# One bank and one place in the queue: value products, post-mix, pre-mix and scores of a talking-heads attention, reordered

## The chip, the cores and the metric

The kernel runs on one core of a Trainium2 chip. The metric is the device time of one execution in microseconds (us), the median of several runs. The kernel before takes 1507.99 us (three runs, 1506.14 to 1509.37). Times inside the program come from one further execution, recorded by the hardware profiler.

## The reference

Attention with heads mixed before and after the softmax ("talking heads"), followed by a small network that is linear but for one product of two halves:

```
scores = einsum('bhij,hg->bgij', q @ k^T / 8, w_pre)      # 8 batches, 12 heads, 448 x 448, head size 64
attn   = exp(scores - max) / (sum + 1e-9)
out    = einsum('bhij,hg->bgij', attn, w_post) @ v
x      = out as (8*448) x 768
result = (((x @ w1) * (x @ w2)) @ w3) @ w_out             # 768 -> 1024 -> 1024 -> 768
```

## The kernel before, in words

**Four products of the attention.** TensorE is used here as four 64 x 64 quadrants: two halves of its rows (the contraction) by two halves of its columns (the output partitions). A 4-byte float matmul shows in the profile as two instructions, so each product below counts twice there.

- *Scores* (`qk`, matmuls at L173): raw scores of a pair of heads, 128 queries by 448 keys; 8 instructions of 448 columns into two PSUM banks, 0 and 1 (6 and 7 for a second unit in one step). ScalarE copies the two banks out (L178, L179; in the first batch VectorE takes some) and SyncE stores them to DRAM (L184, L187). There the layout is changed: `fetch` (L201) reads rows back with (query, head) on the partitions.
- *Pre-mix* (`mix`, L219): a block of 5 queries x 12 heads = 60 partitions is multiplied with a 60 x 60 matrix that holds w_pre; 8 instructions of 448 columns into banks 2 and 3. One "set" is four such blocks, 20 queries; the 8 batches make 180 sets. VectorE takes the extreme of each row (`largest`, L226), ScalarE the exponential (`exp`, L234), both from banks 2 and 3.
- *Post-mix* (`post`, L259): the exponentials, 64 keys at a time, are the stationary operand, and the moving one is a 60 x 60 matrix with w_post and the softmax's denominators (`scale`: VectorE L243 and L244, GpSimd L246). 448 keys are seven tiles of 64. Key tile j of a block goes to PSUM partitions 0 to 63 where j is even and to 64 to 127 where j is odd, that is, to one column half of TensorE or the other. With two halves s of a set's queries and two blocks c that makes 28 products, 56 instructions of 60 columns, into banks 4 and 5, which hold 4 pairs of tiles (NJ = 4). The upper partitions beside the seventh tile are set to zero once, at the start (L781). ScalarE copies banks 4 and 5 out (`put`, L273) into `mt`, with the keys on the partitions.
- *Value products* (`av`, L300): `mt` times v, for 150 queries (a third of a batch) and three pairs of heads: 48 instructions of 150 columns (148 in the last third), which use all 128 rows and one column half each, into one bank, number 2. A batch has six such groups of three, the program 48. The padded v has 512 rows, with zeros in the last 64. In the third to eighth batch ScalarE copies the bank out (`leave`, L307, tile xd) and the result goes to DRAM; in the first two (`ONE = 2`) it is split at once into a rounded part (ScalarE, L321, tile xh) and a rest (VectorE, L322, tile xl).

**The network.** TensorE's remaining work, instructions of 128 x 128 by 448 columns in banks 6 and 7 (L359, L521, L552, L701), is dealt out over the steps by a table (`shares`), so that each step has about as much work on TensorE. It is called the experts' work below, as in the code.

**The order of the work** is written out by hand, and each engine runs its own instructions in that order. The loop in `run` makes half steps n; a set m has an even one (n = 2m: extremes, exponential) and an odd one (denominators). An odd half step's TensorE work is: experts, then value products if they are due (`avs`, in six of a batch's 22 or 23 odd steps), then a score unit if one is due (`qks`, in nearly all odd steps while a later batch is to come), then `post(m-1)`, then `mix(m+1)`, and then the next half step's experts. What leaves PSUM is put on lists: `ends` are run by `do_ends()`, `soon` by `do_soon()`, `later` (mostly DMAs) at the start of the next half step. `bank(i)` runs `ends` and `soon` first if something on them still has to read bank i. Score copies are issued inside `qk` itself; the copy out of the value products' bank is issued by the `do_ends()` that follows the value products and the scores.

All DMAs are issued by SyncE, in order. In an even half step `fetch` comes first, then what stands on `later`.

Of the kernel before, what the change touches and what calls it, by code (L numbers as in the profile page):

```python
# [6 lines left out]
F32 = mybir.dt.float32  # L7
# [3 lines left out]
ALU = mybir.AluOpType  # L11
# [4 lines left out]
B, H, S, D = 8, 12, 448, 64  # L16
DM, FF = 768, 1024
HP = H // 2
IB = 10
GI = H * IB  # L20
NB = -(-S // IB)
QT, NJ = 128, 4
GB = 15
# [3 lines left out]
HK = H * IH  # L27
PP = 64
JB = S // PP
# [20 lines left out]
class Kernel:  # L50
# [198 lines left out]
    def post(self, m):  # L249
        nc, w2s = self.nc, self.w2s.pop(m)  # L250
        if any(b in (4, 5) for b, _ in self.ends):
            self.do_ends()
        for s, e in enumerate(self.es.pop(m)[0]):
            for j in range(JB):
                a, z = divmod(j, 2)
                at = (2 * a + s) * HK
                for c in range(2):
                    k = slice(c * PP, c * PP + HK)
                    nc.tensor.matmul(self.pso[c][z * PP:(z + 1) * PP, at:at + HK], e[k, j * PP:(j + 1) * PP], w2s[k, s],  # L259
                                     start=True, stop=True)  # L260
        for c in range(2):
            n = 2 * m + c
            w, (b, t) = self.width(n), divmod(n, NB)
            a, u = divmod(t, GB)
            if u == 0:
                self.mt[b, a] = self.mp.tile([128, NJ, H, GB * IB], F32, tag="mt", name=f"mt{b}_{a}")
            src = self.pso[c][:, :NJ * 2 * HK].rearrange("p (j s g i) -> p j s g i", j=NJ, s=2, g=H)
            dst = self.mt[b, a][:, :, :, u * IB:u * IB + w]
            self.ends.append((4 + c, lambda dst=dst, src=src, w=w: self.put(dst, src, w)))
# [21 lines left out]
    def av(self, b, a, g):  # L291
        nc, cols = self.nc, self.cols(a)
        W = cols.stop - cols.start
        if g % 3 == 0:
            self.psa = self.bank(2, f"psa{b}_{a}_{g}")[:, :3 * GB * IB].rearrange("p (g i) -> p g i", g=3)
        v, mt = self.vs[b, g], self.mt[b, a]
        for j in range(NJ):
            for s in range(2):
                rows = slice(s * D, (s + 1) * D)
                nc.tensor.matmul(self.psa[rows, g % 3, :W], v[:, j, rows], mt[:, j, 2 * g + s, :W],  # L300
                                 start=(j == 0), stop=(j == NJ - 1))
        if g % 3 == 2 and b >= ONE:
            q, dst = self.psa[:, :, :W], self.x_d[b][g // 3][:, :, cols]
            x = self.xq.tile([128, 3, GB * IB], F32, tag="x", name=f"xd{b}_{a}_{g}")[:, :, :W]

            def leave():
                nc.scalar.copy(x, q)  # L307
                self.later.append(store)

            def store():  # L310
                nc.sync.dma_start(dst, x)
                self.x_made[b] += 1

            self.ends.append((2, leave))
        elif g % 3 == 2:
            if b not in self.xs:
                pool = self.xp[b % 2]
                self.xs[b] = [pool.tile([128, K1, S], F32R, tag=f"x{t}", name=f"x{t}{b}") for t in "hl"]
            h, l = (x[:, g - 2:g + 1, cols] for x in self.xs[b])
            q = self.psa[:, :, :W]  # L320
            self.ends.append((2, lambda: nc.scalar.copy(h, q)))  # L321
            self.soon.append((2, lambda: nc.vector.tensor_tensor(l, q, h.bitcast(F32), op=ALU.subtract)))  # L322
        if a == NG - 1:
            self.later.append(self.load_v)

# [414 lines left out]
    def run(self):  # L740
        nc, tc = self.nc, self.tc
# [36 lines left out]
        self.wpo = cp.tile([128, HK], F32, name="wpo")  # L778
        self.pso = [self.ps.tile([128, 512], F32, tag=f"b{4 + c}", name=f"pso{c}") for c in range(2)]
        for p in self.pso:  # L780
            nc.vector.memset(p[PP:, (NJ - 1) * 2 * HK:NJ * 2 * HK], 0.0)  # L781
        nc.sync.dma_start(self.wpo, self.wpost)
        fold_pieces = self.converting(self.fold_jobs())
        next(fold_pieces)
# [17 lines left out]
        loads, qks, avs = {}, {}, {}  # L802
# [83 lines left out]
        for n in range(N + 6):  # L886
            self.step, third = n, False
            if n == GB + 1:
                self.close("qp")
                self.xp = [self.pool("xp0", 1)]  # L890
            if n == SWITCH:
                assert done == total
                next(background, None)
                self.do_ends()
                self.do_soon()
                self.do_later()
                assert not fold_pieces
                self.close("fp")
                self.wp = self.pool("wp", 5, side="right")
                self.up = self.pool("up", 1, side="right")  # L900
                self.xp.append(self.pool("xp1", 1, side="right"))
                background, total, done = self.experts(phases), (E_1 + E_2) * ONE + P_1 * (B - ONE) // 2, 0
            if n == LATE:
                assert done >= E_1
                self.close("xp0", "cx")
                self.xq, self.cb = self.pool("xq", 2), self.pool("cb", 1)
            if n == PAIR:

                assert done >= 2 * E_1 + E_2 and unit_pieces is None and not self.jobs and not self.ys
                self.do_ends()  # L910
                self.do_soon()
                self.do_later()
                self.pairs, self.w_ahead = True, 4
                self.close("xp1", "cb", "xq", "cs")
                self.xq = self.pool("xq", 2)
                self.up2 = self.pool("up2", 1, side="right")
                self.free += range(N_UP, NS)
                setup = self.pair_setup(phases)
            if PAIR <= n < PAIR + 7:
                next(setup, None)  # L920
            m, odd = divmod(n, 2)
            if not odd and LF <= n + LF < N:
                self.fetch(m + LF // 2)
            self.do_later()
            if n + 3 < HP:
                others(n + 3)
            elif HP <= n < 2 * HP:
                self.load_v()
            for x in loads.get(n, []):
                self.load_kq(*x)  # L930

            p, pieces = self.n_made - 1 if fold_pieces else 2 * KF + 3 * KF, None
            if avs.get(n):
                pass
            elif fold_pieces:
                f = (self.n_made - 1 - 2 * KF) // 3
                if f < 2 or done >= 2 * KF * 3 * (f - 1):
                    pieces = fold_pieces
                    if next(pieces, self) is self:
                        fold_pieces = pieces = None  # L940
            if m < SETS:
                if odd:
                    self.scale(m)
                else:
                    self.largest(m)
            self.do_soon()
            if pieces:
                next(pieces)
            elif unit_pieces and not fold_pieces and not avs.get(n):
                ahead = 1 if n < SWITCH else 2 * done // (3 * K1) + 4 + (done > 0)  # L950
                if n_pieces < ahead:
                    n_pieces += 1
                    if next(unit_pieces, self) is self:
                        unit_pieces = None
                    else:
                        next(unit_pieces)
                        third = True
            now = share.get(n, 0)
            if n < SWITCH:

                wanted += now
                now = max(min(there(p), KF * 3 + wanted) - done, 0)
            self.do_sums()

            advance(now // 2)
            self.do_ends()
            if not odd and m < SETS:
                self.exp(m)
            advance(now - now // 2)
            for x in avs.get(n, []):  # L970
                self.av(*x)
            for i, x in enumerate(qks.get(n, [])):
                self.later.append(self.qk(*x, (6, 7) if i else (0, 1)))
            self.do_ends()
            if odd and 1 <= m <= SETS:
                self.post(m - 1)
            if odd and m + 1 < SETS:
                self.mix(m + 1)
            self.do_ends()
            if third:  # L980
                next(unit_pieces)

# [28 lines left out]
def layouts(inputs):  # L1011
# [4 lines left out]
    kq = np.ascontiguousarray(np.stack([qt.reshape(B, HP, 2 * D, S), kt], axis=3))  # L1016
    q0 = qt[0].reshape(HP, 2 * D, S)
    kq0 = np.ascontiguousarray(np.concatenate([q0[:, :, :QT], kt[0], q0[:, :, QT:]], axis=2))
    vv = np.zeros((B, HP, 2, NJ * 128, D), np.float32)
    vv[:, :, :, :S] = v.reshape(B, HP, 2, S, D)  # L1020
    vv = vv.reshape(B, HP, 2, NJ, 128, D).transpose(0, 1, 4, 3, 2, 5).reshape(B, HP, 128, NJ, 128)
    wpre = np.zeros((128, PP), np.float32)
    wpost = np.zeros((128, HK), np.float32)
# [26 lines left out]
```

## Time and profile before

| | |
|---|---|
| median of the runs | 1507.99 us |
| the profiled execution's own time | 1513.4 us |
| its span in the profile | 1511.6 us |
| TensorE matmuls busy | 1410.9 us, 93% |
| VectorE, ScalarE, GpSimd busy | 738.5, 831.1, 616.5 us |
| data moved | 416.85 MB, 276 GB/s in the mean |
| value products L300 | 2304 instructions, 292 ns each in the mean |
| post-mix L259 | 10080 instructions, 223 ns each |
| pre-mix L219 | 1440 instructions, 570 ns each |

How to read it: PE is TensorE's matmul queue, PEld its loading of stationary operands (which overlaps it), DVE is VectorE, ACT ScalarE, POOL GpSimd, SPq SyncE's queue of DMA issues. Instructions on PE overlap: the duration of one is from its start to its modelled end, and the pace is read from the distance of starts. In a timeline a row merges consecutive instructions of a line: start, length of the merged stretch, engine, line, operation, tiles, shape, count, and in brackets the idle time before it with what ended it. In the view of waits a row says who waited for whom: microseconds in total, times, longest.

### The profile page before, as it was taken

How to read it: one execution, taken by the hardware profiler on the slowest of the kernel's cores; microseconds unless marked ns; L12 is line 12 of the kernel's file. 1: busy time of each engine (PE TensorE's matmuls, PEld its weight loads, DVE VectorE, ACT ScalarE, POOL GpSimd, SP SyncE). 2: the span in 40 equal slices, each digit the busy share in tenths (PEclk: the TensorE clock that was granted, in tenths of full speed). 3: DMA queues.
4: the chain of work that ended last, by engine and by line, in shares of the span. 5: the costliest groups of instructions: out<-in, count | busy, mean ns of one | idle time of the engine just before them, and what ended most of it. 6: DMA issues, size and time to landing. Idle time of an engine off the chain costs nothing.

```text
span 1511.6 us, 45676 instructions
## 1 busy us (share of the span) xinstructions
PE 1410.9 (93%) x18684; PEld 1062.8 (70%) x18684; DVE 738.5 (49%) x1495; ACT 831.1 (55%) x1952; POOL 616.5 (41%) x754
## 2 busy tenths in 40 slices
PE   4869997999899989999999999999999999999999
PEld 1447775666677667667677777777777777899988
DVE  4756565667535443532334343443344447335573
ACT  3766565677656656665555665565555446532231
POOL 1322232344324444531243434543344337446683
PEclk8889999999999999999999999999999999999999
DMA  8988788898889998999988987889878757588875
GB/s 261 345 280 253 226 256 270 289 331 271 298 277 339 323 347 293 353 319 313 316 254 256 309 287 237 258 265 328 294 252 270 229 185 233 180 302 273 255 233 171
DMA packets 203759, 416.85 MB, mean 276 GB/s; under 512 B 20528, under 2 KB 120112, under 8 KB 203472
## 3 DMA queue, kind: packets, MB, share of 16 engines
q1 hardware_dynamic: 203552, 413.94, 83.7%
q8 instruction: 148, 2.42, 0.7%
q14 instruction: 59, 0.48, 0.1%
HBM read 279.77 MB, written 134.09 MB: 274 GB/s over the span
## 4 chain that ended last, share of the span: by engine, by line
PE 65%; DMA 13%; ACT 8%; issue 7%; DVE 5%; SPq 1%; POOL 0%; ACTq 0%; DVEq 0%; POOLq 0%
PE e L701 18%; PE psm L219 9%; PE psq L173 6%; PE pso L259 6%; PE psa L300 6%; PE psf L359 4%; PE e2o L701 4%; PE e3o L701 3%; PE eo L552 3%; PE e1o L701 3%; PE eg L521 3%; DMA wu<-w_d 2%; DMA raw_d<-st 2%; DMA s_d<-s 2%; ACT e L234 2%
## 5 line engine op out<-in xcount | busy, mean ns | idle before, releaser
L226 DVE TENSOR_REDUCE mn<-psm 128x1 f32<-128x448 f32 x360 | 207.9, 620 | 447.1 <-PE psm L219 446.8
L246 POOL TENSOR_SCALAR w<-wpo,ri 128x60 f32<-128x60 f32 x360 | 179.2, 515 | 542.8 <-DVE ri L244 522.0
L701 PE MATMUL e<-eh,wu 128*128 128x448 f32 x1008 | 298.2, 372 | 7.8 <-DVE c L655 4.6
L259 PEld LDWEIGHTS pso<-w,e 60*64 60x64 f32 x10080 | 204.4, 136 | 76.2 <-issue 68.1
L234 ACT ACTIVATE e<-psm,mn 128x448 f32<-128x448 f32 x360 | 226.0, 636 | 50.5 <-DVE mn L226 50.4
L178 ACT COPY st<-psq 128x448 f32<-128x448 f32 x162 | 86.5, 534 | 295.2 <-PE psq L173 135.3
L219 PE MATMUL psm<-r,wsc 60*64 60x448 f32 (+1 forms) x1440 | 199.1, 570 | 51.5 <-ACT xd L307 17.1
L273 ACT COPY mt<-pso 128x480 f32<-128x480 f32 x352 | 201.1, 638 | 67.0 <-PE pso L259 66.9
L701 PEld LDWEIGHTS e<-eh,wu 128*128 128x128 f32 x1008 | 188.0, 188 | 55.6 <-issue 29.5
L259 PE MATMUL pso<-w,e 60*64 60x60 f32 x10080 | 207.7, 223 | 0.5 <-issue 0.5
L701 PE MATMUL e<-el,wu 128*128 128x448 f32 x504 | 187.1, 371 | 0.0
L300 PE MATMUL psa<-mt,v 128*64 128x150 f32 (+1 forms) x2304 | 156.9, 292 | 3.9 <-ACT e L234 3.9
L173 PE MATMUL psq<-kq 64*64 64x448 f32 x1176 | 150.1, 571 | 8.2 <-ACT st L178 8.2
L300 PEld LDWEIGHTS psa<-mt,v 128*64 128x64 f32 x2304 | 143.6, 137 | 19.9 <-issue 9.5
L655 DVE TENSOR_TENSOR c<-c,e 128x448 f32<-128x448 f32 x168 | 101.5, 617 | 66.1 <-PE e L701 61.5
L521 PE MATMUL eg<-xh,wu 128*128 128x448 f32 x384 | 119.7, 381 | 4.3 <-DMA wu<-w_d 4.3
L640 POOL TENSOR_TENSOR el<-x,eh 128x448 fp32r<-128x448 f32 x90 | 104.2, 1176 | 32.7 <-ACT eh L639 29.2
L701 PEld LDWEIGHTS e<-el,wu 128*128 128x128 f32 x504 | 94.8, 188 | 22.7 <-issue 14.1
L521 PEld LDWEIGHTS eg<-xh,wu 128*128 128x128 f32 x384 | 71.8, 190 | 38.3 <-issue 24.2
L219 PEld LDWEIGHTS psm<-r,wsc 60*64 60x64 f32 (+1 forms) x1440 | 50.4, 136 | 65.0 <-ACT xd L307 20.7
L179 ACT COPY st<-psq 128x448 f32<-128x448 f32 x162 | 87.6, 541 | 0.0
L359 PEld LDWEIGHTS psf<-fo,fw 128*128 128x128 f32 x384 | 65.9, 188 | 24.1 <-issue 14.1
(99 smaller groups left out, 1963.1 us busy)
## 6 DMA issues: line engine op xcount, KB each, us to landing
r<-raw_d SPq DMA_DIRECT2D x344, 210.0 KB, 4.1
raw_d<-st SPq DMA_DIRECT2D x138, 448.0 KB, 5.2
wu<-w_d SPq DMA_DIRECT2D x104, 384.0 KB, 6.4
wu<-s_d SPq DMA_DIRECT2D x96, 384.0 KB, 5.0
wu<-w_d SPq DMA_DIRECT2D x51, 512.0 KB, 5.9
kq<-kq SPq DMA_DIRECT2D x42, 448.0 KB, 6.6
wu<-s_d SPq DMA_DIRECT2D x36, 512.0 KB, 5.2
x<-x_d SPq DMA_DIRECT2D x72, 224.0 KB, 6.3
```

The lines of the kernel that those rows point to most:

```text
L173: nc.tensor.matmul(ps[s][z * PP:(z + 1) * PP], t[rows, q:q + PP], t[rows, k:k + S], start=True, stop=True)
L219: nc.tensor.matmul(ps[s][c * PP:(c + 1) * PP, :S], self.wsc[k], r[k, c], start=True, stop=True)
L226: self.nc.vector.tensor_reduce(mn[:, s:s + 1], self.psm[m][s][:, :S], axis=AX.X, op=ALU.min)
L234: nc.scalar.activation(e, p[:, :S], AF.Exp, bias=mn[:, s:s + 1], scale=-1.0, accum_out=sm[:, s:s + 1])
L246: nc.gpsimd.tensor_scalar_mul(w2[:, s], self.wpo, ri[:, s:s + 1])
L259: nc.tensor.matmul(self.pso[c][z * PP:(z + 1) * PP, at:at + HK], e[k, j * PP:(j + 1) * PP], w2s[k, s], start=True, stop=True)
L273: self.nc.scalar.copy(dst.rearrange("p j g (s i) -> p j s g i", s=2), src)
L300: nc.tensor.matmul(self.psa[rows, g % 3, :W], v[:, j, rows], mt[:, j, 2 * g + s, :W], start=(j == 0), stop=(j == NJ - 1))
L359: nc.tensor.matmul(p, w[:, k, x], self.fo[:, k, y, half * DH:(half + 1) * DH], start=(k == 0 and t == 0), stop=(k == KF - 1 and t == 2))
L521: nc.tensor.matmul(p, u[:, k % (K1 // 2), x], xs[y][:, k], start=(k == 0 and t == 0), stop=(k == K1 - 1 and t == 2))
L640: nc.gpsimd.tensor_tensor(lo, x, hi.bitcast(F32), op=ALU.subtract)
L701: nc.tensor.matmul(p, w[:, k, x], ops[m, k][y], start=(k == 0 and t == 0), stop=(k == nk - 1 and t == 2))
```

## The change

1. The value products' bank is number 0, the first of the scores' two, in place of number 2, the first of the pre-mix's two. The entries on `ends` and `soon` name bank 0 accordingly.
2. In a half step the score unit comes last: after post-mix, pre-mix and the `do_ends()` behind them. So the order is value products, post-mix, pre-mix, scores.
3. The seventh key tile (j = 6) of the post-mix goes to the lower column half for s = 0 and to the upper for s = 1 (before: to the lower for both). The zeros beside it are set in two pieces for each bank, and v's last 64 rows stand twice in the padded v in place of the zeros, so that the keys meet their values in either half.

```
             for j in range(JB):
-                a, z = divmod(j, 2)
+                a, z = divmod(j, 2) if j < JB - 1 else (NJ - 1, s)
                 at = (2 * a + s) * HK
...
         if g % 3 == 0:
-            self.psa = self.bank(2, f"psa{b}_{a}_{g}")...
+            self.psa = self.bank(0, f"psa{b}_{a}_{g}")...
...
-            self.ends.append((2, leave))
+            self.ends.append((0, leave))
...
-            self.ends.append((2, lambda: nc.scalar.copy(h, q)))
-            self.soon.append((2, lambda: nc.vector.tensor_tensor(l, q, h.bitcast(F32), op=ALU.subtract)))
+            self.ends.append((0, lambda: nc.scalar.copy(h, q)))
+            self.soon.append((0, lambda: nc.vector.tensor_tensor(l, q, h.bitcast(F32), op=ALU.subtract)))
...
         for p in self.pso:
-            nc.vector.memset(p[PP:, (NJ - 1) * 2 * HK:NJ * 2 * HK], 0.0)
+            for s in range(2):
+                at = (2 * NJ - 2 + s) * HK
+                nc.vector.memset(p[PP * (1 - s):PP * (2 - s), at:at + HK], 0.0)
...
             for x in avs.get(n, []):
                 self.av(*x)
-            for i, x in enumerate(qks.get(n, [])):
-                self.later.append(self.qk(*x, (6, 7) if i else (0, 1)))
             self.do_ends()
             if odd and 1 <= m <= SETS:
                 self.post(m - 1)
             if odd and m + 1 < SETS:
                 self.mix(m + 1)
             self.do_ends()
+            for i, x in enumerate(qks.get(n, [])):
+                self.later.append(self.qk(*x, (6, 7) if i else (0, 1)))
...
-    vv = np.zeros((B, HP, 2, NJ * 128, D), np.float32)
-    vv[:, :, :, :S] = v.reshape(B, HP, 2, S, D)
+    vv = np.concatenate([v, v[:, :, (NJ - 1) * 128:]], axis=2)
```

More of the change, by code (lines that the diff above doesn't have):

```diff
@@ L294, in av @@
         if g % 3 == 0:
-            self.psa = self.bank(2, f"psa{b}_{a}_{g}")[:, :3 * GB * IB].rearrange("p (g i) -> p g i", g=3)
+            self.psa = self.bank(0, f"psa{b}_{a}_{g}")[:, :3 * GB * IB].rearrange("p (g i) -> p g i", g=3)
         v, mt = self.vs[b, g], self.mt[b, a]
```

## The prediction

> **What bounds the kernel.** I read the page's busy shares first, then the windows by stage, then TensorE's waits, then the timelines of four odd half steps, each on TensorE and on the engines it waits for.
>
> ```profile
> span 1511.6 us, 45676 instructions
> PE 1410.9 (93%) x18684; PEld 1062.8 (70%) x18684; DVE 738.5 (49%) x1495; ACT 831.1 (55%) x1952; POOL 616.5 (41%) x754
> PE   4869997999899989999999999999999999999999
> ```
>
> TensorE is busy from the fourth slice of 38 us to the end. What shortens its queue shortens the kernel, unless another engine then becomes the last. Two stages (from, to, length; TensorE, its loads, VectorE, ScalarE, GpSimd busy; clock; DMA share; GB/s):
>
> ```profile
> 260.00:430.00 170.00, 157.91 (x2441) 109.63 (x2440) 109.99 (x231) 120.67 (x290) 65.47 (x91) 0.99 0.89 301
> 430.00:800.00 370.00, 351.29 (x5151) 254.92 (x5151) 152.37 (x325) 216.06 (x516) 139.89 (x176) 0.99 0.93 311
> ```
>
> TensorE idles 170.00 - 157.91 = 12.1 us and 18.7 us there. The waits of the whole span say for whom:
>
> ```profile
> PE psm L219 <- ACT xd L307: 17.1, 27, 0.6
> PE psm L219 <- DVE xl L322: 15.4, 12, 1.3
> PE psm L219 <- DMA r<-raw_d: 11.4, 2, 8.9
> PE psm L219 <- ACT e L234: 7.5, 5, 3.7
> PE psa L300 <- ACT e L234: 3.9, 4, 1.5
> ```
>
> The first two are one thing: pre-mix needs bank 2, which still holds value products. It occurs 27 + 12 = 39 times; the program has 48 groups (2304 instructions, 48 in each). A wait in this view begins when TensorE is dry; what the queue loses is longer and is read from the timelines. From the third batch on, TensorE and then ScalarE:
>
> ```profile
> 745.63 3.28 PE L300 MATMUL psa<-mt,v 128*64 128x150 f32 x48
> 748.84 0.98 PE L173 MATMUL psq<-kq 64*64 64x448 f32 x8
> 749.64 1.10 PE L259 MATMUL pso<-w,e 60*64 60x60 f32 x56
> 751.38 0.98 PE L219 MATMUL psm<-r,wsc 60*64 60x448 f32 x8 [0.64 <-ACT xd L307]
> 752.29 0.47 PE L701 MATMUL e<-eh,wu 128*128 128x448 f32 x1
> ```
>
> ```profile
> 749.92 0.53 ACT L178 COPY st<-psq 128x448 f32<-128x448 f32 x1 [4.23 <-PE psq L173]
> 750.35 0.54 ACT L179 COPY st<-psq 128x448 f32<-128x448 f32 x1
> 750.77 0.55 ACT L307 COPY xd<-psa 128x450 f32<-128x450 f32 x1
> ```
>
> The value products end by 748.91 (745.63 + 3.28), but ScalarE gets to them at 750.77: both score copies stand ahead in its queue, and the first waited for the scores. In the first two batches VectorE's rest comes behind the rounding as well:
>
> ```profile
> 290.26 3.28 PE L300 MATMUL psa<-mt,v 128*64 128x150 f32 x48
> 296.62 1.08 PE L219 MATMUL psm<-r,wsc 60*64 60x448 f32 x8 [1.25 <-DVE xl L322]
> 297.63 0.47 PE L521 MATMUL eg<-xh,wu 128*128 128x448 f32 x1
> ```
>
> ```profile
> 295.94 0.63 DVE L322 TENSOR_TENSOR xl<-psa,xh 128x450 fp32r<-128x450 f32 x1 [3.86 <-ACT xh L321]
> ```
>
> In the last batch there are no score units, and the trace shows value products, post-mix and pre-mix in the new order (TensorE from post-mix on, then ScalarE):
>
> ```profile
> 1235.38 1.09 PE L259 MATMUL pso<-w,e 60*64 60x60 f32 x54
> 1236.26 0.59 PE L219 MATMUL psm<-r,wsc 60*64 60x448 f32 x2
> ```
>
> ```profile
> 1235.50 0.54 ACT L307 COPY xd<-psa 128x450 f32<-128x450 f32 x1 [4.08 <-PE psa L300]
> ```
>
> The copy starts 0.12 us behind post-mix's start and ends at 1236.04, and pre-mix starts 0.88 us behind post-mix's start with no wait. Last, an odd half step without value products:
>
> ```profile
> 662.43 0.98 PE L173 MATMUL psq<-kq 64*64 64x448 f32 x8
> 663.24 1.04 PE L259 MATMUL pso<-w,e 60*64 60x60 f32 x54
> 664.06 0.59 PE L219 MATMUL psm<-r,wsc 60*64 60x448 f32 x2
> 664.11 0.23 PE L259 MATMUL pso<-w,e 60*64 60x60 f32 x2
> 664.17 0.93 PE L219 MATMUL psm<-r,wsc 60*64 60x448 f32 x6
> 665.02 0.47 PE L552 MATMUL eo<-eh,wu 128*128 128x448 f32 x1
> ...
> 670.32 0.59 PE L219 MATMUL psm<-r,wsc 60*64 60x448 f32 x1
> ```
>
> ```profile
> 664.36 1.12 ACT L273 COPY mt<-pso 128x480 f32<-128x480 f32 x2
> 665.35 0.53 ACT L482 CAST s<-y 128x384 fp32r<-128x384 f32 x1
> 665.88 0.64 ACT L234 ACTIVATE e<-psm,mn 128x448 f32<-128x448 f32 x1
> ...
> 666.50 0.63 ACT L234 ACTIVATE e<-psm,mn 128x448 f32<-128x448 f32 x1
> ```
>
> **Part 1, the new order where value products run.** Pieces: value products to next start 748.84 - 745.63 = 3.21; post-mix to pre-mix 0.88 (last batch); pre-mix to scores 0.80, taken from scores to post-mix (749.64 - 748.84), the same eight instructions of 448 columns followed by quadrant work; scores to experts 0.91, taken from pre-mix to experts (752.29 - 751.38), again the same shape. The half step's tail is then 3.21 + 0.88 + 0.80 + 0.91 = 5.80 us. Before it was 752.29 - 745.63 = 6.66 in the later batches and 297.63 - 290.26 = 7.37 in the first two. Saved: 27 x 0.86 = 23.2 and 12 x 1.57 = 18.8, together **42.0 us**.
>
> This needs bank 0 empty when the scores come, 0.88 + 0.80 = 1.68 us behind post-mix's start. The copy is done 0.12 + 0.54 = 0.66 behind it; in the first two batches VectorE's 0.63 makes that 1.29 and a hand-over, which fits. Without that cover, if VectorE is busy just then, it costs a few tenths up to twelve times. I take 0.
>
> **Part 2, the bank at its other end.** Value products no longer wait for an exponential to leave bank 2 (3.9 us, the last row of the waits). They now wait for the score copy from bank 0, which was issued in the half step before; only where value products follow scores almost at once (I expect three such places) is that 0.7 us: the first copy starts 749.92 - 748.84 = 1.08 behind the scores and takes 0.43 to the next start, less the scores' own 0.80. Net 3.9 - 2.1 = **1.8 us** gained; bounds 3.9 - 12 x 0.7 = -4.5 (if the wait came at all twelve groups of the first two batches, when scores also come in even half steps) and 3.9.
>
> **Part 3, the same order elsewhere.** Without value products the tail was 665.02 - 662.43 = 2.59 us; by the pieces above it becomes 0.88 + 0.80 + 0.91 = 2.59. **Nothing**.
>
> **Part 4, the seventh key tile.**
>
> ```profile
> L259 PE MATMUL pso<-w,e 60*64 60x60 f32 x10080 | 207.7, 223 | 0.5 <-issue 0.5
> ```
>
> 10080 / 56 = 180 post-mixes. The lower half of the columns gets 8 of 14 products in each row half, 16 instructions one after another, the upper 6. A whole post-mix lasts 1.10 us (the row at 749.64); less one instruction of 0.22 that is 15 distances, 0.059 us each. Dealt 7 to 7 each column half has 14: two distances less at best. The turn from s = 0 to s = 1 remains, where two products of the lower half meet and the upper half loses a distance, and after it the upper half is the last. I take one distance: 180 x 0.058 = **10.4 us**; bounds 0 and 20.9. The copies out, the value products and v's load have the same sizes as before; the two more memsets at the start are hidden by the first loads.
>
> The Trainium skill ("PSUM — Partial Sum Buffer", section "Engine vs sequencer instructions") speaks against this part: by it matmuls start and complete in program order. The rows at 664.06 and 664.11 say otherwise for quadrants, since two pre-mix instructions start ahead of the last two of the post-mix. By the skill's rule the dealing would be worth nothing and the sum 10.4 us smaller.
>
> **Part 5, what the moved step pushes back.** A score unit is eight matmuls, two ScalarE copies and one store. On ScalarE the copies now stand behind those of banks 4 and 5 and ahead of the next casts and the exponential. In the half step at 662: scores would start at 664.06 + 0.80, their copies 1.08 later at 665.9 and end 2 x 0.43 later at 666.8; the cast of 0.53 behind them, the exponential starts at 667.3 instead of 665.88, 1.4 us late. Without a cast it is some 0.8 late. Both exponentials ended at 666.50 + 0.63 = 667.13; the next pre-mix needs them at 670.32, so 3.2 us cover it here. Where VectorE's extreme is late already, the delay is hidden behind that. I put **5 us** on the half steps with less cover (bounds 0, and the fourth rival). What waits behind the exponential is VectorE's denominators and all that VectorE does next, the experts' sums among it.
>
> ```profile
> SPq L201 <- PE psm L219: 398.7, 113, 8.5
> ```
>
> On SyncE the read-back of r mostly waits for pre-mix, which now comes 0.8 us sooner; the store of the scores behind it finds its copies later, and the network's weights queue behind that by at most about 1 us. They are asked for three or four units ahead. I take 0.
>
> **Part 6, what a faster TensorE meets.** Between 430 and 800 us the DMA engines are already busy 93% of the time, and between 260 and 430 us VectorE 65% and ScalarE 71%, with the conversion of the weights in the same half steps. There a part of the gain will come back as other waits: **5 us** lost, bounds 0 and half of the gain.
>
> Sum: 42.0 + 1.8 + 10.4 - 5 - 5 = 44.2 us. Against the profiled execution's own 1513.4 us (its span 1511.6 and 1.8 around it) that is 1469; this execution lay 5.4 above the median of the runs, so the runs should show **1464 us**.
>
> **The rivals.**
>
> *The wait moves to another resource* (0.18). In favour: DMA at 93% and VectorE and ScalarE at two thirds in the stages where most of the waits lie. Against: in these stages waits for DMA are few (two for r, 11.4 us, most of it one wait of 8.9). Half of the 54 us before the two losses stays: 1508 - 27 = 1481, with 1475 to 1496.
>
> *The dealing is worth nothing*, because the quadrants start in order or the turn costs both distances (0.12): 1508 - 44.2 + 10.4 = 1474.
>
> *Both distances count and nothing comes back* (0.06): 1508 - 42.0 - 1.8 - 20.9 = 1443.
>
> *The exponential becomes the last* (0.04, the slower side). Place: ScalarE in half steps without value products. If two casts and an expert's copy (0.53 each) stand between the score copies and the exponential, it ends 0.80 + 1.08 + 0.86 + 1.6 + 1.25 (667.13 - 665.88) = 5.6 us behind pre-mix's start; the period above is 670.32 - 664.06 = 6.26, and a period under 5.6 would wait. Some 115 half steps have scores and no value products (seven batches of 22 or 23 odd ones, less six in each). The change is undone where each loses 54/115 = 0.47 us on the mean; at 0.6 us it gives 1508 - 54 + 69 = 1523. Against it: at 662 the exponential has 3.2 us to spare.
>
> *The wait stays* (0.02), because something else holds pre-mix after value products as long, r for instance: 1508 - 1.8 - 10.4 + 10 = 1506.
>
> The forecast itself has 0.58, with 1453 to 1473. About 0.2% (3 us) is what a measurement of this kernel can tell from no change. Faster: 0.58 + 0.18 + 0.12 + 0.06, less 0.03 for a first rival that takes back all: 0.91; within 0.2%: 0.03; slower: 0.06. Eight in ten: 1446 to 1489, from near the best case to the middle of the first rival.
>
> **What would show it.** Right: no row of pre-mix waiting for xd or xl; the copy out of bank 0 about 0.1 us behind the value products; tails of about 5.75 us with value products and 2.53 without; post-mix's 56 instructions in about 1.04 us. Wrong: new rows of scores waiting for xd or xl, pre-mix waiting much longer for the exponential or for r, value products waiting for the score copy in more than a few places, or experts waiting longer for weights and sums.

## The result and the profile after

The changed kernel takes 1455.73 us (median of four runs, 1450.72 to 1456.99) against 1508.68 us before (now four runs, 1506.14 to 1512.81): a ratio of 0.964, 95% interval 0.9608 to 0.9672, or 53 us less. The forecast was 1464, with 1453 to 1473.

The page of the changed kernel, its busy shares, and the window of one stage (columns as in the prediction):

```profile
PE 1390.1 (96%) x18684; PEld 1059.4 (73%) x18684; DVE 739.0 (51%) x1497; ACT 833.1 (57%) x1952; POOL 620.7 (43%) x754
...
L259 PE MATMUL pso<-w,e 60*64 60x60 f32 x10080 | 198.6, 224 | 0.1
```

```profile
430.00:800.00 370.00, 358.92 (x5383) 266.04 (x5383) 158.37 (x342) 228.93 (x540) 154.75 (x193) 1.00 0.97 324
```

The profiled execution took 1456.61 us, 56.8 less than that of before. TensorE is busy 96% of a shorter span, and DMA 97% of the stage from 430 to 800 us (93% before). TensorE's waits, the rows that the change touches:

```profile
PE psm L219 <- ACT e L234: 19.9, 15, 5.8
...
PE psq L173 <- ACT st L178: 7.6, 5, 2.6
...
PE psa L300 <- ACT st L178: 1.9, 3, 0.7
```

The two rows of pre-mix waiting for the value products' bank (17.1 and 15.4 us) are gone. The row for the exponential has grown from 7.5 to 19.9 us (13.1 of it in the first 260 us and 3.3 between 480 and 700 us), and value products wait for a score copy in three places, 1.9 us. The scores' own wait for their copies fell from 21.3 us, all of it in the first 100 us, a row of before that the prediction did not use:

```profile
PE psq L173 <- ACT st L178: 21.3, 8, 4.6
```

The half step with value products in a later batch, on TensorE and ScalarE:

```profile
717.17 3.28 PE L300 MATMUL psa<-mt,v 128*64 128x150 f32 x48
720.38 1.08 PE L259 MATMUL pso<-w,e 60*64 60x60 f32 x55
...
722.00 0.98 PE L173 MATMUL psq<-kq 64*64 64x448 f32 x8
722.91 0.67 PE L701 MATMUL e<-eh,wu 128*128 128x448 f32 x2
```

```profile
720.50 0.54 ACT L307 COPY xd<-psa 128x450 f32<-128x450 f32 x1 [2.19 <-PE psa L300]
```

The tail is 722.91 - 717.17 = 5.74 us; it was 6.66. The copy out of the value products' bank starts 0.12 us behind post-mix's start, and the scores find the bank empty. In the first two batches (VectorE's rest below) the tail is 272.31 - 266.57 = 5.74 as well, where it was 7.37:

```profile
266.57 3.28 PE L300 MATMUL psa<-mt,v 128*64 128x150 f32 x48
...
271.40 0.98 PE L173 MATMUL psq<-kq 64*64 64x448 f32 x8
272.31 0.48 PE L521 MATMUL eg<-xl,wu 128*128 128x448 f32 x1
```

```profile
270.47 0.63 DVE L322 TENSOR_TENSOR xl<-psa,xh 128x450 fp32r<-128x450 f32 x1 [0.36 <-ACT xh L321]
```

That rest ends at 271.10, 0.3 us ahead of the scores. A half step without value products, and the pre-mix two sets later:

```profile
628.61 1.08 PE L259 MATMUL pso<-w,e 60*64 60x60 f32 x55
...
631.13 0.47 PE L552 MATMUL eo<-eh,wu 128*128 128x448 f32 x1
...
641.40 1.22 PE L219 MATMUL psm<-r,wsc 60*64 60x448 f32 x5 [0.73 <-ACT e L234]
```

The tail is 631.13 - 628.61 = 2.52 us; it was 2.59. ScalarE ahead of that last row:

```profile
636.86 0.53 ACT L178 COPY st<-psq 128x448 f32<-128x448 f32 x1 [0.44 <-PE psq L173]
637.28 0.54 ACT L179 COPY st<-psq 128x448 f32<-128x448 f32 x1
640.21 0.51 ACT L482 CAST s<-y 128x384 fp32r<-128x384 f32 x1 [2.39 <-DMA s_d<-s]
640.63 0.63 ACT L234 ACTIVATE e<-psm,mn 128x448 f32<-128x448 f32 x1
```

The score copies are done by 637.82, but then a cast of the network's weights waits 2.39 us for a store to free its buffer, with the exponential behind it. Pre-mix waits 0.73 us for it. So a late exponential is not the score copies' work alone.

Last, the start, a place where the prediction expected nothing. The first post-mix on TensorE and the first row of the second, before and after:

```profile
38.56 2.20 PE L173 MATMUL psq<-kqz 64*64 64x448 f32 x8 [3.17 <-ACT st L178]
40.11 2.02 PE L259 MATMUL pso<-w,e 60*64 60x60 f32 x53
...
47.28 0.21 PE L259 MATMUL pso<-w,e 60*64 60x60 f32 x1
```

```profile
34.91 1.09 PE L259 MATMUL pso<-w,e 60*64 60x60 f32 x56
...
45.28 0.91 PE L259 MATMUL pso<-w,e 60*64 60x60 f32 x46
```

Before, post-mix and pre-mix stood behind scores that waited 3.17 us for their banks. After, they go first, and this post-mix starts 5.2 us sooner. At the second one (after, the view ends at 46 us) the lead is down to 2.0 us. Later starts cannot size it: TensorE's granted clock from 35 to 100 us was 0.83 in the profile of before and 0.92 in this one.

### The profile page after: what moved, and what is told of

The parts are those of the page before. It is cut to its first block, busy times and chain, and to the rows that moved or that the text cites. A ratio compares the mean times of both kernels' runs of the same rounds, so it can differ in the third digit from the quotient of the medians.

```text
span 1454.8 us, 45722 instructions
## 1 busy us (share of the span) xinstructions
PE 1390.1 (96%) x18684; PEld 1059.4 (73%) x18684; DVE 739.0 (51%) x1497; ACT 833.1 (57%) x1952; POOL 620.7 (43%) x754
## 4 chain that ended last, share of the span: by engine, by line
PE 78%; DMA 13%; DVE 5%; ACT 3%; issue 1%; SPq 0%; POOL 0%; DVEq 0%; ACTq 0%; POOLq 0%
PE e L701 20%; PE psa L300 10%; PE pso L259 10%; PE psm L219 8%; PE psq L173 7%; PE psf L359 5%; PE eg L521 4%; PE e2o L701 4%; PE e1o L701 4%; PE e3o L701 4%; DMA s_d<-s 3%; PE eo L552 3%; DMA cs<-wo 3%; DMA r<-raw_d 2%; DMA wu<-w_d 2%; ACT e L234 1%
## 5 line engine op out<-in xcount | busy, mean ns | idle before, releaser
L273 ACT COPY mt<-pso 128x480 f32<-128x480 f32 x352 | 197.8, 621 | 177.3 <-PE pso L259 177.1
L219 PE MATMUL psm<-r,wsc 60*64 60x448 f32 (+1 forms) x1440 | 197.9, 557 | 32.1 <-ACT e L234 19.9
L259 PEld LDWEIGHTS pso<-w,e 60*64 60x64 f32 x10080 | 174.5, 134 | 50.0 <-issue 44.0
L259 PE MATMUL pso<-w,e 60*64 60x60 f32 x10080 | 198.6, 224 | 0.1
L173 PE MATMUL psq<-kq 64*64 64x448 f32 x1176 | 159.5, 546 | 0.6 <-ACT st L178 0.6
L243 DVE TENSOR_SCALAR sa<-sm 128x2 f32<-128x2 f32 x180 | 35.9, 200 | 129.6 <-ACT e L234 129.0
L173 PEld LDWEIGHTS psq<-kq 64*64 64x64 f32 x1176 | 62.2, 136 | 53.8 <-issue 29.8
```

The lines of the kernel that those rows point to most:

```text
L173: nc.tensor.matmul(ps[s][z * PP:(z + 1) * PP], t[rows, q:q + PP], t[rows, k:k + S], start=True, stop=True)
L219: nc.tensor.matmul(ps[s][c * PP:(c + 1) * PP, :S], self.wsc[k], r[k, c], start=True, stop=True)
L273: self.nc.scalar.copy(dst.rearrange("p j g (s i) -> p j s g i", s=2), src)
```

## The experiments

Every ratio is to the kernel before on the same chip, with its 95% interval; the changed kernel has 0.9640. The executions of one kernel lie 5 to 16 us apart, so a difference of a few microseconds between two kernels is given with what their intervals allow.

**x1, no dealing.** The changed kernel with the old column halves, memset and padding:

```
-                a, z = divmod(j, 2) if j < JB - 1 else (NJ - 1, s)
+                a, z = divmod(j, 2)
```

> The changed kernel without the dealing (all seventh key tiles in the lower column half again, the new bank and the new order kept). Theory: the dealing takes one distance of 0.058 us out of each of 180 post-mixes, so this kernel is 10.4 us slower than the changed one, about 1466 us, and a half step without value products has a tail of 2.59 us instead of 2.53. Rival, quadrants bound to the program's order: no difference, 1456 us, tails alike. Rival, both distances: 20.9 us, 1477 us.

Measured: 1457.6 us, 0.9670 (0.9644 to 0.9695). The post-mix keeps TensorE busy for 210.1 us instead of 198.6 (the group of L259), and the tails are 2.59 and 5.80 us, as expected. In time it is 4.5 us by the ratios and 2 by the medians, short of the 10.4 forecast, but the intervals overlap, so its size stays open.

**x2, dealing alone** on the kernel before:

```
-                a, z = divmod(j, 2)
+                a, z = divmod(j, 2) if j < JB - 1 else (NJ - 1, s)
```

> The kernel before with the dealing alone. Theory: one distance in each post-mix wherever nothing else holds pre-mix. 39 post-mixes are followed by the wait for the value products' bank, which ends at the same time whatever post-mix takes, so 141 of 180 count: 8 us, 1500 us. Rivals: 0 (1508 us) with the program's order, 16 us (1492 us) with two distances.

Measured: 1507.79 against 1510.04 us, 0.9981 (0.9962 to 1.0): 2.9 us, 0 to 5.7, where 8 was expected. To look for the rest, one pair of profiles: the post-mix of the 61st set and the last one, before and then x2:

```profile
481.10 0.69 PE L259 MATMUL pso<-w,e 60*64 60x60 f32 x34
...
1324.88 0.52 PE L259 MATMUL pso<-w,e 60*64 60x60 f32 x20
```

```profile
484.45 0.63 PE L259 MATMUL pso<-w,e 60*64 60x60 f32 x30
...
1320.80 0.40 PE L259 MATMUL pso<-w,e 60*64 60x60 f32 x12
```

Between these rows lie 119 sets: 843.78 us before and 836.35 in x2, 7.4 less or 0.062 a set, the size of the forecast distance. At the first of them x2 is 3.35 us behind. But the granted clock differs too: it was 0.96 before and 0.94 in x2 up to these rows, and 0.99 and 1.00 between them, and a hundredth of 840 us would be as much as the difference itself. So neither the loss nor the gain in this pair can be put down to the dealing alone; where the rest of the 8 us went is open. The trace shows the 0.06 us itself: the tail without value products is 2.53 us in most half steps of x2, and 2.59 before.

**x3, copy first.** One line in the kernel before:

```
                 self.av(*x)
+            self.do_ends()
             for i, x in enumerate(qks.get(n, [])):
```

> The kernel before with one more line: what stands on the list of ends is run between value products and scores, so that ScalarE copies the value products out ahead of the score copies. Bank 2 and the old order stay. Theory (the wait is ScalarE's queue, two score copies that themselves wait for the scores): the copy is done 0.7 us behind the value products and, in the first two batches, VectorE's rest about 1.4 us behind them, while pre-mix comes 0.80 + 0.83 = 1.63 us behind; no wait is left, 27 x 0.9 + 12 x 1.6 = about 43 us, 1465 us. Rival (the shared bank itself costs the wait, whatever the order on ScalarE): about 1508 us.

Measured: 1469.92 against 1510.04 us, 0.9767 (0.973 to 0.9803): 35 us (30 to 41) of the 53, from four runs that lie 16 us apart. Bank 2 and the old order are kept, and the wait is gone. TensorE and ScalarE in x3:

```profile
712.44 1.04 PE L259 MATMUL pso<-w,e 60*64 60x60 f32 x54
713.26 0.59 PE L219 MATMUL psm<-r,wsc 60*64 60x448 f32 x2
```

```profile
711.75 0.53 ACT L307 COPY xd<-psa 128x450 f32<-128x450 f32 x1 [3.27 <-PE psa L300]
712.71 0.53 ACT L178 COPY st<-psq 128x448 f32<-128x448 f32 x1 [0.43 <-PE psq L173]
```

Pre-mix follows post-mix after 0.82 us, as everywhere else. So the wait was a matter of ScalarE's queue, and the shared bank by itself costs nothing here. The tails with value products are 5.80 us in x3, where 28 took 6.66 and 12 took 7.37, which makes the forecast 43 us in the trace; in time it is above the interval.

**x4, bank 2.** The changed kernel with the value products back in bank 2 (`self.bank(2, ...)` and the three list entries).

> The changed kernel with the value products back in bank 2 (the new order and the dealing kept). Theory (the order on ScalarE is the cause, the bank a help): the copy is done before pre-mix in the later batches; in the first two the rest is done about 1.35 us behind post-mix's start and pre-mix waits 0.5 us twelve times, 6 us; value products wait for the exponential again (3.9 us) and not for the score copy (1.9 us); together 8 us, 1464 us. Rival (the bank is what matters): the waits come back, 1456 + 42 = 1498 us.

Measured: 1461.47 us, 0.9692 (0.9669 to 0.9716), 8 us above the changed kernel by the ratios, as expected; the intervals just touch. Its waits show the first two of the three parts:

```profile
PE psm L219 <- DVE xl L322: 3.0, 11, 0.3
...
PE psa L300 <- ACT e L234: 2.5, 2, 2.2
```

This view counts only the time in which TensorE is dry. The tail in the first two batches is 6.34 us in most half steps, against 5.74 in the changed kernel: 0.60 us twelve times, about 7 us, where 6 was forecast.

**x7, bank 0 with the old order.** The changed kernel with the score units again directly behind the value products.

> The changed kernel with the old order (scores directly behind the value products) and bank 0 and the dealing kept. Theory: the scores now need the bank that the value products have just filled. In the later batches the copy is done about 0.7 us behind the value products and the scores wait that long; in the first two they wait for VectorE's rest, 1.4 us: 27 x 0.7 + 12 x 1.4 = 36 us, of the 42 that the old wait cost, so with the dealing about 1456 + 36 + 5 at the start = 1497 us. Rival (bank 2 was the trouble, another bank suffices): 1456 to 1462 us.

Measured: 1496.09 against 1509.25 us, 0.9899 (0.9862 to 0.9935). The bank alone moves the wait from pre-mix to the scores:

```profile
PE psq L173 <- ACT xd L307: 17.8, 28, 0.7
PE psq L173 <- DVE xl L322: 16.0, 12, 1.8
```

**x5, the turn.** The changed kernel with alternating column halves throughout:

```
-            for j in range(JB):
+            for j in ((1, 0, 3, 2, 5, 4, 6) if s else range(JB)):
```

> The changed kernel with the key tiles of s = 1 issued in the order 1, 0, 3, 2, 5, 4, 6, so that the two column halves alternate through the whole post-mix, over the turn from s = 0 to s = 1 too. Theory (the turn costs the upper half one distance, and it is then the last): one more distance of 0.058 us from each post-mix, 10 us less, about 1445 us; pre-mix starts at the same 0.80 to 0.86 us but the tail without value products falls from 2.53 to 2.47. Rival (fourteen distances are reached already, or the quadrants' loads bind): no difference, 1456 us.

Measured: 1453.41 us, 0.9619 (0.9591 to 0.9646), 3 us less with overlapping intervals, where 10 was forecast. In the trace the post-mix is busy for 191.3 us (198.6), and the tail with value products is 5.71 us instead of 5.74, without them 2.50 instead of 2.53. So the turn costs half a distance, not a whole one, and little of that is time.

**x6, the order by value products.** Scores come first wherever there are no value products:

```
+            for i, x in enumerate([] if avs.get(n) else qks.get(n, [])):
+                self.later.append(self.qk(*x, (6, 7) if i else (0, 1)))
             self.do_ends()
...
-            for i, x in enumerate(qks.get(n, [])):
+            for i, x in enumerate(qks.get(n, []) if avs.get(n) else []):
```

> The changed kernel with the new order only in half steps that have value products; elsewhere the scores come first again, as before the change. Theory of the prediction (score copies ahead of the exponential make it late): pre-mix's wait for the exponential falls from 19.9 back to about 7.5 us, and the time by about 8 us, 1448 us. Rival (the exponential is late because ScalarE stands at casts that wait for DMAs, and DMA is busier because the kernel is faster): that wait stays near 20 us. At the start the old order is back, and what the changed kernel gained before the first value products (6 us) is lost if the order gave it: then 1462 us by the rival.

Measured: 1456.24 us, 0.9643 (0.9619 to 0.9667): no difference, where the theory had 8 us less. Two effects that would cancel show in its waits and its start:

```profile
PE psq L173 <- ACT st L178: 21.3, 9, 3.6
...
PE psm L219 <- ACT e L234: 7.2, 5, 4.7
```

```profile
38.55 2.20 PE L173 MATMUL psq<-kqz 64*64 64x448 f32 x8 [3.56 <-ACT st L178]
40.09 1.18 PE L259 MATMUL pso<-w,e 60*64 60x60 f32 x23
```

The exponential's wait falls from 19.9 to 7.2 us: the score copies do make it late. (Where both the copies and the casts stand as in the changed kernel, this row is 13.3 us in x1, 13.4 in x4 and 19.2 in x5, so only a fall well below 13 says something.) The first post-mix is 5.2 us later than in the changed kernel again.

**y1, both orders.** x6, but with the new order in the first 18 half steps (`n < FOLD or avs.get(n)`).

> As x6 (scores first where there are no value products), but in the first 18 half steps the new order, as in the changed kernel. Theory (the new order gains about 6 us before the first value products, because pre-mix no longer stands behind scores that wait for their banks, and costs about 8 us later, because the score copies stand ahead of the exponential): both are had, 1456 - 6 = 1450 us, and the first post-mix starts at 35 us instead of 40. Rival (time won at the start is lost again to the conversions that follow): 1456 us.

Measured: 1451.31 against 1511.3 us, 0.9599 (0.9569 to 0.963): 6.6 us under x6 by the ratios, with the first post-mix at 35.78 us and the exponential's wait at 9.1 us. This is about the 6 us expected for the start, though the two intervals overlap a little, and the traces do not show a lead that is simply carried along: y1 is 4.3 us ahead of x6 at the first post-mix, 1.1 at the second and 4.8 at the 61st. Against the changed kernel it is 6 us, which would be the price of the score copies' place; these intervals overlap too.

**x8, sums behind the exponential.**

```
-            self.do_sums()
             advance(now // 2)
             self.do_ends()
             if not odd and m < SETS:
                 self.exp(m)
+            self.do_sums()
```

> The changed kernel with the sums of weights (and their casts on ScalarE, which often wait for a store to free a buffer) issued behind the half step's exponential instead of ahead of it. Theory (between 480 and 700 us the exponential is late because such a cast stands ahead of it in ScalarE's queue and waits for a DMA): pre-mix's waits for the exponential in that stretch, about 5 us in six places, go, and the time falls by 3 to 6 us, about 1451 us. Rival (the score copies or VectorE make the exponential late): no difference, 1456 us, or slower if the sums come late for the weights.

Measured: 1445.64 us, 0.9579 (0.9555 to 0.9603), below the changed kernel's interval: 9 us by the ratios, more than the 3 to 6 expected, and 64 us under the kernel before. The wait at which it aimed, pre-mix for the exponential between 480 and 700 us, is 3.3 us in five places in the changed kernel, and x8 has none. The 30 sets from the 71st to the 101st post-mix (from 521 to 727 us in the changed kernel) take 200.1 us, against 202.8 to 206.5 in the changed kernel, x1, x4 and x5. So something that the sums do ahead of the exponential costs time in its own right. The edit also moves the sums' work on VectorE and GpSimd, so the casts that wait for a store are the likely cause, not one shown alone, and what is over the 3 to 6 us is not located. The row of the whole span (12.8 us for 19.9) does not settle it, since x1 and x4 have 13.3 and 13.4 with the sums in their old place.

**y3 and y2, combinations.** y3 is x8 with x5's order of key tiles; y2 is y3 with y1's order.

> The changed kernel with the sums behind the exponential (x8) and alternating column halves (x5). If they add: 1445.6 - 2.5 = about 1443 us. The tail without value products is 2.50 us as in x5.

> The changed kernel with three edits together: sums behind the exponential (x8, 10 us), alternating column halves (x5, 2 to 3 us), and the order of y1 (6 us if it adds). If the three are independent: about 1438 us. If x8 and y1 remove the same lateness of the exponential: about 1443 us.

Measured: 1448.35 us, 0.9573 (0.9545 to 0.9601), and 1448.19 us, 0.9575 (0.9549 to 0.9601). Both miss their forecasts by 5 us or more, and neither is better than x8. This fits the second theory of y2, that x8 and y1 remove the same lateness; the turn adds nothing that these runs can tell.

**y4, the exponential first.** The changed kernel with `exp(m)` directly behind the extremes, ahead of conversions, sums and the experts' copies:

```
             self.do_soon()
+            if not odd and m < SETS:
+                self.exp(m)
             if pieces:
...
-            if not odd and m < SETS:
-                self.exp(m)
             advance(now - now // 2)
```

> The changed kernel with the exponential issued directly behind the row extremes in the even half step, ahead of the conversions' squares, the weights' casts and the experts' copies on ScalarE. Theory (whatever stands ahead of the exponential on ScalarE and waits for a DMA makes it late; the squares, that wait for loads of weights, are the larger part): pre-mix's wait for the exponential falls below 6 us, and the time below x8's, 1440 us. Rival (the experts' copies and the conversions' squares are needed sooner than the exponential): the wait falls, but VectorE's conversions or the experts wait in its place, 1446 us or more.

Measured: 1456.07 us, 0.9627 (0.96 to 0.9654): as the changed kernel. The wait it aimed at is down to 7.9 us, but others have come; VectorE's conversions now wait for the squares on ScalarE (2.1 us in the changed kernel):

```profile
DVE cx L120 <- ACT cm L106: 19.0, 21, 1.6
```

So the rival holds: some of what stands ahead of the exponential is needed sooner than it. x8 moves only the sums.

## Why the prediction was right, point by point

**Part 1 (42.0 us) was right in mechanism, and in size as far as the tails go.** The tails were forecast at 5.80 us before the dealing's 0.06 and measured 5.74, in both kinds of batches, with no wait for bank 0. x3 shows the cause: ScalarE's queue, in which the copy stood behind two copies that waited for the scores. x7 and x4 show that order and bank differ in weight: the new bank without the order gives 15 us with the dealing, the order without the bank gives all but 8. What x3 gives in time, 35 us (30 to 41), is under the 43 us of its tails, so the kernel did not keep all of it.

**Part 2 (1.8 us) was right to the place:** 3.9 us of waits went, and 1.9 us came in three places.

**Part 3 (nothing) missed the start.** Its working held for the steady half step (2.59 and, with the dealing, 2.52 us). It took that as the whole, and did not look at the first half steps, where scores wait for their own banks and everything behind them on TensorE waits too. The row for it (21.3 us of scores waiting for their copies) stood in the view of waits and was left unused. Its worth is 6.6 us in time by y1 against x6, with intervals that overlap; in the traces a lead of 5.2 us at the first post-mix is 2.0 at the second, so how it comes to that time is open.

**Part 4 (10.4 us) was right in the trace and mis-sized in time.** Each post-mix does lose one distance (busy time 207.7 to 198.6 us, tails by 0.06 us). In time x1 gives 2 to 4.5 us, with overlapping intervals, and x2 2.9 (0 to 5.7), which excludes the 8 forecast for it. The working took each distance as time of the whole kernel although its own Part 6 held that TensorE is not the last engine everywhere. Where the rest went is not settled.

**Part 5 (a loss of 5 us) named a real cause and half of it.** The score copies' place costs about 6 us by y1, with overlapping intervals, and the wait for the exponential is 12.7 us longer than in x6. But a second thing is there: casts in front of the exponential that wait for DMAs (2.39 us at 640 us), which the working had counted only by their 0.5 us of duration. Putting the sums behind the exponential (x8) gives 9 us, moving the score copies back (y1) 6, and both together (y2) no more than x8.

**Part 6 (a loss of 5 us) was not measured by itself.** That something takes gains back is shown by x3, where 43 us of shorter tails gave 30 to 41 us of time, and by x2; x1 and x5 point the same way within their intervals.

In sum, 42 + 2 for the value products, 3 to 4 for the dealing, 5 to 6 for the start and 6 lost to the exponential make about 47 of the 53 us measured (49 to 59 by the interval). With the 35 us of x3 in place of the 42 they make about 40. So 6 to 13 us are not assigned. That the sum of 44 came within 9 us of the time is in part luck: the dealing gave 6 to 8 us less than its term, and the start, which had no term, gave time in its place. The fourth rival, the exponential as the last, did show up as a wait, at about a ninth of the price that would have undone the change. The rival by the rule on program order that the prediction cites from the Trainium skill falls: the tail without value products is 2.59 us in most half steps of x1, 2.53 with the dealing and 2.50 with x5's order, as quadrants that run side by side would have it.

## What to carry to other kernels

When an engine waits for a buffer, look at what stands ahead of the releasing instruction in its own engine's queue before giving the buffer a new place: here one line that reordered ScalarE's copies gave two thirds of the gain. An instruction that may wait for a DMA and is not needed soon is better placed behind one that another engine waits for (9 us in x8); what is needed sooner than that one is not (nothing gained in y4). Instructions saved on an engine that is busy 93% of the span need not all come out as time (x2 gave 0 to 5.7 us for 8), so such savings should be sized stage by stage, the first microseconds among them.

## What the runs showed of the hardware that was not expected

Instructions in different quadrants of TensorE do not always start in program order, even across two products. In the changed kernel at 382 us pre-mix waits for bank 2 and then bank 3, and the first score instruction, later in the program, starts ahead of three of pre-mix:

```profile
382.42 1.22 PE L219 MATMUL psm<-r,wsc 60*64 60x448 f32 x5 [1.76 <-ACT e L234]
383.22 0.54 PE L173 MATMUL psq<-kq 64*64 64x448 f32 x1
383.46 0.55 PE L219 MATMUL psm<-r,wsc 60*64 60x448 f32 x3
```

The Trainium skill ("PSUM — Partial Sum Buffer", section "Engine vs sequencer instructions") has matmuls start and complete in program order. This trace does not agree: the score instruction starts 0.24 us early, and the measurement decides for quadrants of this shape.

The granted clock of TensorE differs between executions of one program, and the time with it. Of the eleven executions of the kernel before that ran beside y1 to y4, the four longest (1516.6 to 1518.7 us) had 0.974 to 0.980, and the other seven (1507.5 to 1513.6 us) 0.982 to 0.986. Two profiles should be compared with their clocks beside them.
